# The tiles of running maxima of units 1 to 3, initialised by VectorE in place of GpSimd

## The chip, the cores and the metric

The kernel runs on one core of one Trainium2 chip. The metric is the device time in microseconds of one execution; the median of several executions is given, and one more execution is recorded by the hardware profiler. TensorE (PE in the profile) multiplies matrices, VectorE (DVE) reduces and does elementwise work, ScalarE (ACT) evaluates functions and copies, GpSimd (POOL) does elementwise work on the on-chip memory, and SyncE's queue (SP) issues the DMAs. Each engine works through its own queue in order, and engines wait for each other by semaphores.

## The reference

A transformer block with adaptive layer normalisation, in float32, for 2048 tokens of width 448, with 16 heads of 28:

```python
mod = (silu(c) @ w_mod).reshape(1, 6, 1, -1)            # sa, ca, ga, sb, cb, gb
h = layernorm(x) * (1 + ca) + sa
q, k, v = split_heads(h @ wqkv)                          # 16 heads, Dh = 28
p = softmax(q @ k^T * Dh ** -0.5)                        # per head, 2048 x 2048
x = x + ga * ((p @ v) @ wo)
h = layernorm(x) * (1 + cb) + sb
y = layernorm(h)
x = x + gb * (gelu(y @ w1 + b1) @ w2 + b2)               # 448 -> 1792 -> 448
```

## The kernel before

Every large product is made from two parts of each operand, a rounded one ("hi") and the remainder ("lo"), in three matmuls. The 16 heads are four groups `g` of four heads, and the 2048 tokens are four blocks `b` (or `qt` for queries, `cch` for keys) of 512. A **unit** is one pair (g, qt), number 4 g + qt: the attention of four heads for 512 queries.

The softmax needs the largest score of each query before the exponentials. The kernel computes these in a pass of its own: for a unit, a query row block `i`, a head `j` and a key block `cch` there is one matmul 128 x 512 (`max_mm`, line 544), and VectorE reduces its result to one column of the tile `mxp` of that unit, [128, 4, 4, 4] float32, 64 elements per partition (`max_one`, line 549). When all are there, `max_fin` reduces `mxp` over the key blocks (line 589). The tile is set to -3.0e38 when the unit's first matmul is written (lines 538 to 541); unit 0's is not.

For units 1 to 3 (`paired`) the key blocks 0 and 1 go together, in `pair_diff`: with the difference of the two key blocks (`k_diff`, tile `raw`) one matmul gives the difference of scores, ScalarE takes its positive part into a tile `slot_d`, `slot_d0h` or `slot_d0i` (line 557), a second matmul gives the scores of block 0, and one VectorE instruction adds the two and takes the maximum (line 561, in the profile a custom instruction and a read of its accumulator into `mxp`).

The **first phase**, up to about 170 us, goes over the token blocks `b` (line 894). For each, TensorE runs tasks of eleven matmuls (line 464): queries or keys of one group (`qk_task`, result `pa`), then four tasks of values (`v_task`, weights `slot_e`), then the queries and keys of group 0 of the next block. After each task comes a group of matmuls for maxima (`emit_task`, line 764), four to six of them, in five or six PSUM buffers named `ma`, `m` and `o`. In between, ScalarE copies results out (lines 500 and 526) and rounds them (503), and GpSimd subtracts for the remainder (507), which the DMA queue sends off (510). For the next block's input, GpSimd normalises transposed rows (`xn`, lines 333 and 334), ScalarE applies scale and shift (361, into a buffer `full`, of which there are three) and rounds (345), and GpSimd makes the remainder (347 and 349). These operands are `slot_b` for block 2 and `slot_c` for block 3. The second phase runs attention proper (lines 1408, 1453, 1466), the last the output projection and the MLP.

The order on every engine is the order in which the program is written, and the pools decide which buffer a tile gets.

Of the kernel before, what the change touches and what calls it, by code (L numbers as in the profile page):

```python
# [47 lines left out]
def tile_adaln_block(ctx: ExitStack, tc: tile.TileContext, x, x_t, wqkv, wo, w1, b1, w2, b2, c, w_mod, out):  # L48
    nc = tc.nc
    pe, act, dve, pool, sp = nc.tensor, nc.scalar, nc.vector, nc.gpsimd, nc.sync  # L50
# [31 lines left out]
    def sbt(tag, shape, dt=F32, bufs=1):  # L82
        return sb.tile(shape, dt, tag=tag, name=nm(tag), bufs=bufs)
# [445 lines left out]
    mxp = {}  # L529
# [4 lines left out]
    paired = ((0, 1), (0, 2), (0, 3))  # L534
    px_no = [0]

    def max_mm(g, qt, i, j, k, ps=None):
        if (g, qt) not in mxp:
            mxp[(g, qt)] = sbt("mxp", [128, 4, 4, 4], bufs=6)
            if (g, qt) != (0, 0):  # L540
                (pool if (g, qt) in paired else dve).memset(mxp[(g, qt)], -3.0e38)
        m = (ps or ps_mx)()
        js = slice(32 * j, 32 * j + DH)
        pe.matmul(m, qh_sb[(g, qt)][js, i * 128 : (i + 1) * 128], k[js, :], start=True, stop=True)  # L544
        return m

    def max_one(g, qt, cch, i, j, ps=None):
        m = max_mm(g, qt, i, j, kh_sb[(g, cch)], ps)
        dve.tensor_reduce(out=mxp[(g, qt)][:, i, j, cch : cch + 1], in_=m, op=ALU.max, axis=AX.X)  # L549
# [3 lines left out]
    def pair_diff(g, qt, i, j):  # L553
        m = max_mm(g, qt, i, j, k_diff[0])
        r = d0(1 + px_no[0] % 3)
        px_no[0] += 1
        act.activation(r, m, AF.Relu)

        def rest(ps):
            m = max_mm(g, qt, i, j, kh_sb[(g, 0)], ps)  # L560
            dve.tensor_tensor_reduce(
                out=r, in0=m, in1=r, scale=1.0, scalar=-3.0e38, op0=ALU.add, op1=ALU.max,
                accum_out=mxp[(g, qt)][:, i, j, 1:2],
            )

        return rest
# [849 lines left out]
    for u in range(NU):  # L1416
        g, qt = divmod(u, NB)
# [193 lines left out]
```

## Time and profile before

| | us |
|---|---|
| median of 3 runs | 1093.62 (1092.92 to 1094.41) |
| profiled execution | 1093.22 |
| its span, first to last instruction | 1091.4 |
| TensorE busy | 1079.4 (99%) |
| VectorE busy | 800.5 (73%) |
| ScalarE busy | 691.8 (63%) |
| GpSimd busy | 251.7 (23%) |

The page lists for each engine its busy time, then forty slices of the span in tenths (with `PEclk`, the clock granted to TensorE), then the chain that ended last: the work followed back from the last instruction, at each step to what released it. A row of the timeline gives start, duration, engine, line, operation, and the tiles as out<-in; in brackets the idle time of the engine before it and the releaser. Times in a row of a stretch are its length and each engine's busy time in it (PE, PEld, DVE, ACT, POOL), then the clock, the DMA share and GB/s.

### The profile page before, as it was taken

To read this page: it belongs to the slowest core of one execution; us is meant where nothing else is said; L and a number is where in the kernel's file an instruction comes from. 1 tells how busy PE (TensorE), PEld (TensorE's weight loads), DVE (VectorE), ACT (ScalarE), POOL (GpSimd) and SP (SyncE) were. 2 spreads that over 40 slices of the span, in tenths; PEclk is the share of its full clock that TensorE was granted. 3 is DMA by queue.
4 is the path that set the end of the run, shared out by engine and by line. 5 is a ranking of instruction groups with operands and counts; after the bars stand their busy time and mean duration, and the time that the engine had idled before them with its cause. 6 is when DMAs were issued, how large, how long until landed. Compare 5 with 4: busy or idle time off the path is not lost.

```text
span 1091.4 us, 20645 instructions
## 1 busy us (share of the span) xinstructions
PE 1079.4 (99%) x8199; PEld 657.1 (60%) x8199; DVE 800.5 (73%) x1371; ACT 691.8 (63%) x870; POOL 251.7 (23%) x231
## 2 busy tenths in 40 slices
PE   8999899999999999999999999999999999999998
PEld 6766675444444444444444444544488888888887
DVE  6978688989989898988888988585745565464322
ACT  4645658888888888888888888687943321211111
POOL 1584630011011011025231410216114032061000
PEclk9999899999999999999999999999999999999999
DMA  9454262122121311143322423111343301102000
GB/s 314 171 185 128 78 207 87 44 65 57 51 76 51 87 28 58 53 121 96 95 65 78 128 64 99 57 32 56 115 130 96 104 35 40 34 34 73 34 1 34
DMA packets 60759, 91.73 MB, mean 84 GB/s; under 512 B 14159, under 2 KB 26086, under 8 KB 60650
## 3 DMA queue, kind: packets, MB, share of 16 engines
q1 hardware_dynamic: 60178, 89.67, 26.6%
q8 instruction: 64, 1.05, 0.4%
q10 hardware_dynamic: 148, 0.46, 0.1%
q14 instruction: 33, 0.27, 0.1%
q0 software_dynamic: 336, 0.28, 0.1%
HBM read 62.54 MB, written 29.51 MB: 84 GB/s over the span
## 4 chain that ended last, share of the span: by engine, by line
PE 95%; DVE 2%; DMA 1%; ACT 1%; issue 1%; POOL 1%; SPq 0%; ACTq 0%; POOLq 0%; DVEq 0%
PE s L1453 24%; PE o L1408 23%; PE m L464 16%; PE pa L464 8%; PE m L544 7%; PE s L1545 3%; PE s L1547 3%; PE s L1546 3%; PE s L544 2%; PE ma L544 1%; DVE mxp L549 1%; PE t L1547 1%; PE t L1545 1%; PE t L1546 1%; DMA slot_c<-in_w_mod_dram 1%
## 5 line engine op out<-in xcount | busy, mean ns | idle before, releaser
L549 DVE TENSOR_REDUCE mxp<-m 128x1 f32<-128x512 f32 x583 | 376.3, 686 | 76.5 <-PE m L544 59.6
L1453 PE MATMUL s<-slot_b,slot_a 28*128 28x512 f32 (+1 forms) x3072 | 358.4, 425 | 0.1
L1453 PEld LDWEIGHTS s<-slot_b,slot_a 28*128 28x128 f32 (+1 forms) x3072 | 211.5, 183 | 175.2 <-ACT slot_c L1466 97.4
L544 PE MATMUL m<-kh,qh 28*128 28x512 f32 x607 | 221.6, 472 | 0.4 <-ACT full L840 0.3
L1466 ACT ACTIVATE slot_c<-s 128x1024 f32<-128x1024 f32 x170 | 174.8, 1028 | 52.3 <-PE s L1453 51.3
L1408 PE MATMUL o<-slot_c,v 128*32 128x512 f32 x680 | 178.9, 605 | 0.0
L1501 ACT ACTIVATE full<-m,b_col 128x512 f32<-128x512 f32 x56 | 38.6, 690 | 193.5 <-PE m L464 193.5
L757 DVE TENSOR_REDUCE mxp<-s 128x2 f32<-128x1024 f32 x107 | 131.2, 1226 | 5.7 <-PE s L544 0.8
L1408 PE MATMUL o<-slot_c1h,v 128*32 128x512 f32 x512 | 134.7, 605 | 0.0
L1408 PE MATMUL o<-slot_c0h,v 128*32 128x512 f32 x508 | 133.6, 605 | 0.0
L1466 ACT ACTIVATE slot_c1h<-s 128x1024 f32<-128x1024 f32 x128 | 130.7, 1021 | 0.0
L1466 ACT ACTIVATE slot_c0h<-s 128x1024 f32<-128x1024 f32 x127 | 130.6, 1028 | 0.0
L1466 ACT ACTIVATE slot_d<-s 128x1024 f32<-128x1024 f32 x86 | 88.4, 1028 | 27.0 <-PE s L1453 26.3
L1128 POOL TENSOR_TENSOR osb<-osb,osb 128x512 f32<-128x512 f32 x16 | 20.6, 1286 | 343.3 <-DMA osb<-drec 306.2
L544 PEld LDWEIGHTS m<-kh,qh 28*128 28x128 f32 x607 | 88.5, 182 | 15.5 <-DVE mxp L549 13.0
L1504 DVE CAST hi<-full 128x512 fp32r<-128x512 f32 x42 | 19.1, 455 | 101.7 <-ACT full L1501 101.7
L1408 PE MATMUL o<-slot_d,v 128*32 128x512 f32 x344 | 90.5, 605 | 0.4 <-ACT osb L1372 0.4
L1505 DVE TENSOR_TENSOR lo<-full,hi 128x512 fp32r<-128x512 f32 x56 | 46.2, 825 | 29.3 <-ACT hi L1504 25.3
L464 PE MATMUL m<-y,slot_a 128*128 128x512 f32 x160 | 59.7, 389 | 0.0
L721 DVE CUSTOM_DVE_ANT_0 slot_d0i<-m,slot_d0i 128x512 f32<-128x512 f32 x55 | 38.0, 692 | 16.2 <-PE m L544 12.2
L1408 PEld LDWEIGHTS o<-slot_c,v 128*32 128x32 f32 x680 | 24.5, 108 | 39.8 <-issue 37.9
L544 PE MATMUL s<-kh,qh 28*128 28x512 f32 x214 | 47.2, 436 | 0.0
(366 smaller groups left out, 1827.5 us busy)
## 6 DMA issues: line engine op xcount, KB each, us to landing
slot_b<-d SPq DMA_DIRECT2D x32, 256.0 KB
slot_a<-d SPq DMA_DIRECT2D x32, 256.0 KB
d<-lo SPq DMA_DIRECT2D x28, 256.0 KB
d<-hi SPq DMA_DIRECT2D x16, 256.0 KB
osb<-drec SPq DMA_DIRECT2D x15, 256.0 KB
out_dram<-xn SPq DMA_DIRECT2D x16, 224.0 KB
raw<-in_B_w_dram SPq DMA_DIRECT2D x14, 224.0 KB
qh<-d SPq DMA_DIRECT2D x12, 256.0 KB
```

The source lines that it names most:

```text
L464: pe.matmul(p, a, b, start=(i == 0), stop=(i == len(terms) - 1))
L544: pe.matmul(m, qh_sb[(g, qt)][js, i * 128 : (i + 1) * 128], k[js, :], start=True, stop=True)
L549: dve.tensor_reduce(out=mxp[(g, qt)][:, i, j, cch : cch + 1], in_=m, op=ALU.max, axis=AX.X)
L757: dve.tensor_reduce(out=mxp[(g, qt)][:, i, j : j + 2, cch], in_=t, op=ALU.max, axis=AX.X)
L1408: pe.matmul(o[32 * j : 32 * j + 32, :], v_sb[kt // 4][:, kt % 4, 4 * g + j, :], p[j // 2][:, j % 2, :], start=(kt == 0), stop=(kt == NKT - 1),
L1453: pe.matmul(s2[:, jj, :], ks[rows_, kp, kc], qs[rows_, qp, :], start=(term == 0), stop=(term == 2))
L1466: act.activation(pt[hf], s2, AF.Exp, scale=SCALE)
L1501: act.activation(gf, p, AF.Gelu_apprx_tanh, bias=b1_col[:, i : i + 1])
L1505: dve.tensor_tensor(out=glo, in0=gf, in1=f(ghi), op=ALU.subtract)
L1545: pe.matmul(pp, ghi[:, ts], w_hi, start=(m == 0), stop=False)
L1546: pe.matmul(pp, ghi[:, ts], w_lo, start=False, stop=False)
L1547: pe.matmul(pp, glo[:, ts], w_hi, start=False, stop=(m == NFT - 1))
```

## The change

`max_mm` sets the tile `mxp` of every unit but 0 with VectorE; before, it used GpSimd for units 1 to 3.

```diff
@@ max_mm
         if (g, qt) not in mxp:
             mxp[(g, qt)] = sbt("mxp", [128, 4, 4, 4], bufs=6)
             if (g, qt) != (0, 0):
-                (pool if (g, qt) in paired else dve).memset(mxp[(g, qt)], -3.0e38)
+                dve.memset(mxp[(g, qt)], -3.0e38)
```

Three instructions move from one queue to the other. The middle one is that of unit 2 (g = 0, qt = 2), its tile `mxp_1370`, at the last query task of block 2. On GpSimd it stands between the subtractions for two tasks:

```order
 L334 TENSOR_TENSOR xn_1090<-xn_1090,slot_v_295_1231 128x512
 L507 TENSOR_TENSOR lo_1348<-full_1347,hi_1346 128x512
-L541 MEMSET mxp_1370 128x64
 L507 TENSOR_TENSOR lo_1392<-full_1391,hi_1390 128x512
 L333 TENSOR_TENSOR xn_1130<-xn_1130,slot_v_295_1231 128x512
```

GpSimd goes from one subtraction straight to the next. On VectorE, with what each instruction waits for in brackets (`Pool`, `PE`, `Activation` and `DVE` are the semaphores of GpSimd, TensorE, ScalarE and VectorE), the place is the group of maxima in which unit 2 begins:

```order
 L561 ISA slot_d_18_101,mxp_817<-o_1343,slot_d_18_101 128x512 [waits PE_49,Activation_49]
 L561 ISA mxp_817 128x1
+L541 MEMSET mxp_1370 128x64
 L549 TENSOR_REDUCE mxp_433<-m_330_1378 128x1 [waits PE_49]
 L549 TENSOR_REDUCE mxp_433<-m_331_1381 128x1 [waits PE_49]
-L561 ISA slot_d0h_102,mxp_1370<-ma_1384,slot_d0h_102 128x512 [waits PE_49,Activation_49,Pool_49]
+L561 ISA slot_d0h_102,mxp_1370<-ma_1384,slot_d0h_102 128x512 [waits DVE_49,PE_49,Activation_49]
 L561 ISA mxp_1370 128x1
```

The memset stands at the head of the group, two reductions ahead of the first instruction that writes the tile of unit 2, and that instruction waits for VectorE's own semaphore in place of GpSimd's. The rows of TensorE, ScalarE and the DMA queue are the same in both kernels. In the two groups of maxima after this one, and at the first value task of block 2 between them, some of TensorE's waits for a PSUM buffer name another engine than before:

```order
 L544 MATMUL m_341_1421<-kh_291_1215,qh_73_341 128x512 [waits DVE_49]
-L544 MATMUL ma_1424<-kh_87_379,qh_278_1165 128x512 [waits Activation_49]
+L544 MATMUL ma_1424<-kh_87_379,qh_278_1165 128x512 [waits DVE_49]
 L544 MATMUL o_1427<-kh_87_379,qh_278_1165 128x512 [waits DVE_49]
-L464 MATMUL pa_1453<-slot_e_38_144,slot_b_228_961 128x448
+L464 MATMUL pa_1453<-slot_e_38_144,slot_b_228_961 128x448 [waits Activation_49]
```

Here the second `ma` of the group after waits for VectorE where it waited for ScalarE.

## The prediction, written before the changed kernel ran

> **What bounds the kernel now.** I read the page's busy times first, then its slices and the chain that ended last.
>
> ```profile
> span 1091.4 us, 20645 instructions
> PE 1079.4 (99%) x8199; PEld 657.1 (60%) x8199; DVE 800.5 (73%) x1371; ACT 691.8 (63%) x870; POOL 251.7 (23%) x231
> PEclk9999899999999999999999999999999999999999
> PE 95%; DVE 2%; DMA 1%; ACT 1%; issue 1%; POOL 1%; SPq 0%; ACTq 0%; POOLq 0%; DVEq 0%
> ```
>
> TensorE sets the end: it is busy 99% of the span and holds 95% of the chain. So an edit on VectorE and GpSimd counts only where TensorE waits, or runs slow, because of it. One slice of 27 us, the fifth (109 to 136 us), has a lower granted clock than its neighbours, and one of the three removed memsets lies in it. The groups of the edited line show all fifteen memsets.
>
> ```profile
> L541 DVE MEMSET mxp<- x12: 112/112/112, 43.2 to 682.2; 128x64 f32 x12
> L541 POOL MEMSET mxp<- x3: 147/147/148, 60.5 to 143.2; 128x64 f32 x3
>   DVE slot_d0h L561: 3.9, 1
> ```
>
> Twelve already run on VectorE at 0.112 us, three on GpSimd at 0.147 us, and VectorE waited 3.9 us for one of the three. The chain of waits in order of time shows what that did:
>
> ```profile
> 109.02 1.25 POOL lo L507
> 110.27 1.26 POOL xn L333
> ...
> 111.61 1.27 POOL xn L334
> 112.87 1.22 POOL lo L507
> 114.09 0.10 POOL mxp L541
> ...
> 114.22 0.04 DVE slot_d0h L561
> ...
> 114.92 0.60 DVE slot_d0i L561
> ...
> 115.58 0.79 PE o L544
> ```
>
> GpSimd is here behind with its queue: four elementwise operations of about 1.25 us stand directly ahead of a memset that itself needs no data. That memset, of the tile of unit 2, releases VectorE, and VectorE releases TensorE. The timeline of that stretch, engine by engine:
>
> ```profile
> 108.96 0.60 ACT L557 ACTIVATE slot_d0h<-ma 128x512 f32<-128x512 f32 x1 [1.16 <-PE m L544]
> 109.03 1.29 DVE L549 TENSOR_REDUCE mxp<-m 128x1 f32<-128x512 f32 x2 [0.87 <-PE m L544]
> 111.80 0.49 PE L544 MATMUL ma<-raw,qh 28*128 28x512 f32 x1
> 112.97 0.50 PE L544 MATMUL ma<-kh,qh 28*128 28x512 f32 x1 [0.67 <-ACT slot_d L557]
> 114.03 0.15 POOL L541 MEMSET mxp<- 128x64 f32 x1
> 114.22 0.69 DVE L561 CUSTOM_DVE_ANT_0 slot_d0h<-ma,slot_d0h 128x512 f32<-128x512 f32 x1 [3.90 <-POOL mxp L541]
> 115.58 0.79 PE L544 MATMUL o<-kh,qh 28*128 28x512 f32 x1 [2.11 <-DVE mxp L561]
> ```
>
> TensorE idles 0.67 + 2.11 = 2.78 us. The stall has a second part, seen in the granted clock by short windows (the last three columns are clock, DMA share and GB/s):
>
> ```profile
> 114.25:114.50 0.25, 0.00 (x0) 0.00 (x0) 0.25 (x1) 0.00 (x0) 0.25 (x1) 1.00 0.00 0
> 114.75:115.00 0.25, 0.00 (x0) 0.00 (x0) 0.25 (x3) 0.00 (x0) 0.25 (x1) 0.50 0.17 66
> 121.00:121.25 0.25, 0.25 (x4) 0.20 (x2) 0.00 (x0) 0.00 (x0) 0.25 (x1) 0.50 0.57 213
> 121.50:122.00 0.50, 0.50 (x5) 0.30 (x2) 0.40 (x1) 0.47 (x1) 0.50 (x1) 1.00 0.15 57
> ```
>
> The clock falls to 0.50 between 114.50 and 114.75, during the idle time, and is back after 121.25: some 6.7 us at half rate.
>
> **The change, part by part.** *The wait for the memset of unit 2.* I price it from the distance between the groups of matmuls for the maxima, each of which opens with one `ma<-raw`; between two groups lies one task of TensorE.
>
> ```profile
> 120.71 0.79 PE L544 MATMUL ma<-raw,qh 28*128 28x512 f32 x1
> 124.12 0.49 PE L544 MATMUL ma<-raw,qh 28*128 28x512 f32 x1
> 127.20 0.49 PE L544 MATMUL ma<-raw,qh 28*128 28x512 f32 x1
> 130.30 0.49 PE L544 MATMUL ma<-raw,qh 28*128 28x512 f32 x1
> ```
>
> Undisturbed, a value task with its maxima takes 3.08 to 3.10 us (124.12 to 127.20 to 130.30). The two from 111.80 to 124.12 are of the same kind and took 12.32 us, 6.14 more than 2 x 3.09. Of the 6.14, 2.78 are the idle time. The rest is half rate: from 115.58 to about 121.4 TensorE works 5.8 us for 2.9 us of matmuls, and some 0.4 us is left for refilling.
>
> After the change nothing of GpSimd holds the VectorE instruction that ran at 114.22. Its other two sources are the matmul `ma`, in a group opened one task earlier, and ScalarE's `slot_d0h`, done at 108.96 + 0.60 = 109.56. The new wait on VectorE's own memset is met as the memset now stands ahead of the two reductions of 109.03, where VectorE is idle 0.87 us, so its 0.112 us is hidden there (without that cover it costs 0.11). The reductions end about 110.3, the two L561 instructions about 111.6, before the 111.80 group, which then goes through without a pause. The whole 6.14 us is on the path, so the gain is 6.14 if nothing else is late.
>
> *What is late next.* GpSimd does not get earlier: its backlog only shrinks by the memset, 0.15 us at most. TensorE comes 6.14 us earlier, to the query task whose operands GpSimd still makes:
>
> ```profile
> 122.11 1.29 POOL L334 TENSOR_TENSOR xn<-xn,slot_v 128x512 f32<-128x512 f32 x1
> 124.48 1.29 POOL L347 TENSOR_TENSOR slot_c<-full,slot_c 128x512 fp32r<-128x512 f32 x1 [1.08 <-ACT slot_c L345]
> 127.61 1.28 POOL L347 TENSOR_TENSOR slot_c1h<-full,slot_c0h 128x512 fp32r<-128x512 f32 x1 [1.83 <-ACT slot_c0h L345]
> 130.74 1.29 POOL L349 TENSOR_TENSOR slot_c0h<-full,slot_c0h 64x512 fp32r<-64x512 f32 x1 [1.84 <-ACT slot_c0h L345]
> 133.15 0.62 PE L464 MATMUL pa<-slot_c0h,slot_a 128*128 128x512 f32 x2
> ```
>
> Before, GpSimd finished the normalisation of the last chunk at 123.40 and then idled ahead of each remaining step, waiting on ScalarE. Run without gaps, from 123.3, the three steps of about 1.25 us end at 127.0. TensorE's matmul on the last of them, at 133.15, moves to 133.15 - 6.14 = 127.0. They meet: a loss of 0 to 0.3 us, and I take 0.1. The gaps of 1.08, 1.83 and 1.84 us on GpSimd are thus what pays for the gain; were they not there, 4.75 us of it would be lost. ScalarE has to feed these steps:
>
> ```profile
> 124.12:127.20 3.08, 3.08 (x18) 2.28 (x17) 2.48 (x6) 2.80 (x6) 1.29 (x1) 1.00 0.00 0
> ```
>
> In an undisturbed task it is busy 2.80 of 3.08 us (the fourth column after the length), so it keeps up. It starts late, though:
>
> ```profile
> 115.97 0.82 ACT L361 ACTIVATE full<-xn,cols 128x512 f32<-128x512 f32 x1
> 117.20 0.63 ACT L345 CAST slot_c<-full 128x512 fp32r<-128x512 f32 x1
> ```
>
> The buffer `full` of this first chunk comes free only when GpSimd's operation of 112.87 ends, at 114.09. The chunk's work on ScalarE, 115.97 to 117.83, is then done at about 116.0, some 0.6 us after the point at which the next group (near 114.9) wants ScalarE. At 0.28 us of slack a task that is made up within three tasks; a group's buffers are wanted again only 3.1 us later, so the lag eats slack and not the path.
>
> *The memsets of units 1 and 3.* On VectorE they add 0.112 us each, in front of idle time:
>
> ```profile
> 65.15 0.69 DVE L549 TENSOR_REDUCE mxp<-ma 128x1 f32<-128x512 f32 x1 [1.37 <-PE m L544]
> 144.41 1.89 DVE L549 TENSOR_REDUCE mxp<-m 128x1 f32<-128x512 f32 x3 [0.32 <-PE m L544]
> ```
>
> The first run of reductions is followed by 1.37 us of idle time, and the third memset falls into the 0.32 us. Each is hidden; exposed, together, they would cost 0.22 us. What GpSimd saves there, 0.15 us each, nobody waits for: only one wait for a memset is on record. Bounds of these two: -0.3 to +0.22, taken as 0. No DMA, matmul or order on TensorE, ScalarE or the DMA queue changes, so all that follows 127 us moves forward as a block.
>
> **Sum.** -6.14 + 0.1 = -6.0 us. The profiled execution took 1093.22 us (span 1091.4), which becomes 1087.2. It lies 0.40 below the median of the three runs, 1093.62, so the predicted median is 1087.6. Runs differ by 1.5 us (1092.92 to 1094.41); 0.2%, about what a measurement of this kernel tells from no change, is 2.2 us.
>
> **A rule against the full gain.** In the rows the clock fell after 0.67 and 2.11 us of idle time, broken by one matmul. The Trainium skill, "TensorE: Matmul & The Clock Gate", section "HAM oscillation — how this bites in real kernels", has it that gaps must exceed about 3.4 us before the clock is throttled. By that rule these gaps would not be the cause, and the half rate would come regardless; the rows disagree, since the clock falls inside the gap and in no other slice, so I let the measurement decide and keep the rule's case as a rival.
>
> **The rivals.**
> - *GpSimd is the next bound.* It works without a gap from 109 us on and meets TensorE with no slack at 127.0. If its steps start 1 to 2 us later than I put them (ScalarE late with one of the three, or a buffer released late), TensorE idles that long: gain 4 to 5 us, 1088.6 to 1089.6. For it: the lack of slack. Against: the gaps of 1.83 and 1.84 us were waits for ScalarE work that TensorE's own delay had made late. Chance 0.13.
> - *The half rate stays.* Only the 2.78 us of idle time goes: 1090.8. For it: no second such drop shows cause and effect. Against: the clock fell within the gap. Chance 0.04.
> - *Another wait takes its place, or the edit doesn't take effect.* 1093.6. Against: the other sources were ready 4.6 us before, and the order has no memset left on GpSimd. Chance 0.05.
> - *Slower.* GpSimd is late for the query task at 127.0 by so much that TensorE idles as long as now (2.78 us) and its clock halves again: 2.78 + 3.36 us, all of the gain. From a delay of 2.8 us on the kernel is slower, by about the excess; a delay of 6 us would give 1096.8. That needs GpSimd's ten or so operations between 114 and 127 us to take a fifth longer each, which no row hints at. Chance 0.03.
>
> **How the numbers follow.** My forecast, the full gain, has 0.75. Faster by over 0.2% are it, the GpSimd case and the half-rate case: 0.92. Within 0.2%: 0.05. Slower: 0.03. The range goes below by the runs' spread and GpSimd's 0.15 (1086.6) and above takes in the GpSimd case with the spread (1090.0).
>
> **What would show it.** Right: VectorE's L561 no longer waits for L541; TensorE has no idle time at 112 to 116 us; the granted clock reads 1.00 through the fifth slice; groups 3.1 us apart from 111.8 on; the query task's first matmul near 124.8 in place of 130.96. Wrong: a new idle time of TensorE around 127 us with GpSimd's L349 as its releaser, or a half-rate stretch at another place.

## The result, and the profile after

| us | before | after |
|---|---|---|
| median, 6 runs each | 1093.93 (1092.92 to 1095.36) | 1087.82 (1086.50 to 1089.13) |
| profiled execution | 1093.22 | 1088.08 |
| span | 1091.4 | 1086.3 |

The ratio is 0.9944, with a 95% interval of 0.9931 to 0.9957: 6.1 us less. The page of the changed kernel, its totals and the clock by slices:

```profile
span 1086.3 us, 20646 instructions
PE 1077.9 (99%) x8199; PEld 656.5 (60%) x8199; DVE 801.0 (74%) x1374; ACT 691.2 (64%) x870; POOL 251.2 (23%) x228
PEclk9999999999999999999999999999999999999999
```

VectorE has three instructions more and GpSimd three fewer, by 0.5 us each way, and the fifth slice of the clock is a 9 like its neighbours. The edited line, and then the place of the old stall in the timeline of VectorE and TensorE:

```profile
L541 DVE MEMSET mxp<- x15: 112/112/112, 43.5 to 677.2; 128x64 f32 x15
```

```profile
108.33 0.11 DVE L541 MEMSET mxp<- 128x64 f32 x1
109.24 1.29 DVE L549 TENSOR_REDUCE mxp<-m 128x1 f32<-128x512 f32 x2 [0.80 <-PE m L544]
110.45 0.68 DVE L561 CUSTOM_DVE_ANT_0 slot_d0h<-ma,slot_d0h 128x512 f32<-128x512 f32 x1
112.01 0.49 PE L544 MATMUL ma<-raw,qh 28*128 28x512 f32 x1
115.10 0.49 PE L544 MATMUL ma<-raw,qh 28*128 28x512 f32 x1
118.20 0.49 PE L544 MATMUL ma<-raw,qh 28*128 28x512 f32 x1
121.29 0.49 PE L544 MATMUL ma<-raw,qh 28*128 28x512 f32 x1
124.40 0.49 PE L544 MATMUL ma<-raw,qh 28*128 28x512 f32 x1
127.89 0.73 PE L464 MATMUL pa<-slot_c0h,slot_a 128*128 128x512 f32 x2 [0.46 <-POOL slot_c0h L349]
128.55 0.50 PE L544 MATMUL ma<-raw,qh 28*128 28x512 f32 x1
```

The memset runs in 0.11 us where VectorE waits for TensorE anyway, and the first L561 follows the reductions at once. The groups stand 3.09 to 3.11 us apart from 112.01 to 124.40, where before the first two steps took 12.32 us. Then TensorE has the wait at GpSimd's L349.

Against the rows of before the gain can be followed group by group. Both profiles reach the group of unit 2's second step nearly together (111.80 before, 112.01 after). The one that stood at 124.12 is at 118.20, 5.92 us earlier, 6.13 counted from the group at 112. The one at 130.30 is at 124.40, 5.90 earlier. The next one stood here:

```profile
133.69 0.49 PE L544 MATMUL ma<-raw,qh 28*128 28x512 f32 x1
```

It is now at 128.55, 5.14 earlier, and 5.1 is what the span has gained. So of 6.13 us, 0.76 were given back at GpSimd's next late step, and 0.21 is the later start. The medians, 6.1 us apart, are of runs whose spread is 2.4 to 2.6 us.

### The profile page after: what moved, and what is told of

It is laid out like the page before. It is cut to its first block, busy times and chain, and to the rows that moved or that the text cites. A ratio compares the mean times of both kernels' runs of the same rounds, so it can differ in the third digit from the quotient of the medians.

```text
span 1086.3 us, 20646 instructions
## 1 busy us (share of the span) xinstructions
PE 1077.9 (99%) x8199; PEld 656.5 (60%) x8199; DVE 801.0 (74%) x1374; ACT 691.2 (64%) x870; POOL 251.2 (23%) x228
## 4 chain that ended last, share of the span: by engine, by line
PE 87%; ACT 0%; issue 0%; DVE 0%; ACTq 0%
PE s L1453 24%; PE o L1408 23%; PE m L464 17%; PE m L544 6%; PE s L1545 3%; PE s L1547 3%; PE s L1546 3%; PE pa L464 2%; PE s L544 2%; PE t L1547 1%; PE t L1545 1%; PE t L1546 1%; PE ma L544 0%; PE m L340 0%; DVE mxp L549 0%
```

## The experiments

Each kernel was timed beside the kernel before on the same chip. In three of them unit 2's memset, the engine and the place in the queue are told apart.

**Unit 2 alone on VectorE.**

```diff
-(pool if (g, qt) in paired else dve).memset(mxp[(g, qt)], -3.0e38)
+(pool if (g, qt) in ((0, 1), (0, 3)) else dve).memset(mxp[(g, qt)], -3.0e38)
```

> Only the memset of unit 2 goes to VectorE; those of units 1 and 3 stay on GpSimd. Theory A (the memset of unit 2 stood behind a backlog on GpSimd and held VectorE and TensorE): the whole gain, 6 us below the kernel before, 1087.6 to 1088.2, with no wait for L541 and the clock at 1.00 through 109 to 136 us. Rival B (GpSimd relieved of work, or VectorE's memset being the cheaper, 0.035 us each): a third of the gain or less, 1092 or more.

Measured: 1087.41 us against 1093.41, ratio 0.9945 (0.9932 to 0.9959). The whole gain. In its profile two memsets are on GpSimd as before, VectorE waits for neither, and TensorE has the same small wait for L349 (0.43 us). Rival B falls.

**Units 1 and 3 on VectorE, unit 2 on GpSimd.**

```diff
+(pool if (g, qt) == (0, 2) else dve).memset(mxp[(g, qt)], -3.0e38)
```

> Only the memsets of units 1 and 3 go to VectorE; that of unit 2 stays on GpSimd. Theory A: no change beyond 0.3 us, the wait of 3.9 us and the half-rate stretch stay. Rival B: two thirds of the gain, some 4 us.

Measured: 1093.94 against 1093.41, ratio 0.9999 (0.9990 to 1.0008). Nothing. Its profile has the stall again, and larger, from the lists of waits of VectorE and TensorE:

```profile
DVE slot_d0h L561 <- POOL mxp L541: 5.7, 1, 5.7
PE o L544 <- DVE mxp L561: 4.0, 1, 4.0
PE ma L544 <- ACT slot_d L557: 0.7, 1, 0.7
```

**All three on GpSimd, but early.** The tiles of units 1 to 3 are made and set when unit 0's is made.

```diff
+for n in [(0, 0), *paired] if (g, qt) == (0, 0) else [(g, qt)]:
+    mxp[n] = sbt("mxp", [128, 4, 4, 4], bufs=6)
+    if n != (0, 0):
+        (pool if n in paired else dve).memset(mxp[n], -3.0e38)
```

> All three memsets stay on GpSimd, but are issued when the tile of unit 0 is made, near 30 us, far ahead of the backlog. Theory A (the place in the queue matters and not the engine): the whole gain, 1087.6 to 1088.3. Rival B (the engine matters): no gain, 1093.9. Rival C (the gain comes from the waits that changed with VectorE's new instruction): no gain either.

Measured: 1088.29 against 1093.41, ratio 0.9953 (0.9939 to 0.9966). The gain is there with GpSimd doing the work (the line number is one higher in this kernel):

```profile
L542 POOL MEMSET mxp<- x3: 147/147/147, 33.2 to 33.4; 128x64 f32 x3
```

So the place in the queue made the stall, and not the engine. Rivals B and C fall.

**Where GpSimd's backlog comes from.** The kernel before, with the statistics of the last block's normalisation one task earlier; no memset is moved.

```diff
-n_stat = n - (7, 6, 99)[b]
+n_stat = n - (7, 5, 99)[b]
```

> The kernel before, memsets on GpSimd as they were, but the statistics of the last block's normalisation one task earlier, so that the rows GpSimd waits for (4.6 us of idle time until 106.4 us) are sent off before the keys of group 0 and come some 3 us earlier. Theory A (GpSimd's backlog, which starts at that wait, is what made the memset late): the memset comes near 111 us, VectorE waits under 1 us for it, no half-rate stretch, and most of the gain appears with no memset moved: 1087.2 to 1089. Rival B (the engine of the memset matters): no gain, 1093.4 or so.

Measured: 1087.27 against 1093.19, ratio 0.9938 (0.9925 to 0.9950), all of the gain. GpSimd's first normalising step, which waited until 106.36 before, and VectorE's wait for the memset:

```profile
102.72 1.30 POOL L333 TENSOR_TENSOR xn<-xn,slot_v 128x512 f32<-128x512 f32 x1 [1.41 <-DMA slot_v<-ln_dr]
110.45 0.15 POOL L541 MEMSET mxp<- 128x64 f32 x1
110.64 0.69 DVE L561 CUSTOM_DVE_ANT_0 slot_d0h<-ma,slot_d0h 128x512 f32<-128x512 f32 x1 [1.43 <-POOL mxp L541]
```

The rows and the memset come 3.6 us earlier (2.5 counted from the groups of this profile, which itself runs 1.1 us ahead there). A wait of 1.43 us in place of 3.90 leaves TensorE one listed pause of 0.20 us and the clock at full rate; the group concerned takes 1.1 us longer than undisturbed (110.68 to 114.89), and TensorE does not wait for L349 afterwards. VectorE's wait was expected under 1 us; that was a miss, and it cost the 1.1 us of this group, though the time fell within the range expected. Theory A holds: the DMA that GpSimd waited for made the backlog, and the backlog made the memset late.

**Filling TensorE's idle time.** The kernel before, with the wait kept and nine matmuls put where TensorE idled longest.

```diff
 for x, op in enumerate(ops):
+    if fill[0] and x == len(ops) - 1:       # last query task of block 2
+        held.append(ps_s())                 # the next value task's buffer
+        for _ in range(9):
+            pe.matmul(held[0], wq[0][0](0)[:, 0:128], hT[2][0](0), start=True, stop=True)
     op(...)
```

> The kernel before, with the wait kept, and nine matmuls of 0.225 us put on TensorE ahead of the last matmul of the group at 111.8 us, where it idled 2.11 us; their result is overwritten. Theory A with the half rate caused by the idle time: the clock stays at 1.00, the 2.78 us are still lost (as idle time or as filling), and the half rate's 3.36 us are gained: 1090.3 to 1090.9 against 1093.9. Rival D (the half rate comes regardless of the idle time): the clock drops all the same, and the time is 1093.9 or a little more.

Measured: 1092.01 against 1093.41, ratio 0.9991 (0.9981 to 1.0001): 1.4 us by the medians and 1.0 by the ratio, where 3.0 to 3.6 were expected, and not clear of no change. The stretch of 109 to 136 us, in the filled kernel and then in the kernel before (sixth number after the length: the clock):

```profile
109.00:136.00 27.00, 26.09 (x134) 18.09 (x134) 17.54 (x42) 17.82 (x32) 20.00 (x19) 1.00 0.23 86
```

```profile
109.00:136.00 27.00, 24.22 (x111) 17.12 (x110) 16.75 (x39) 17.35 (x32) 18.03 (x18) 0.87 0.21 79
```

Whether the half rate comes from the idle time is settled by this: VectorE still waits 4.3 us for the memset, TensorE still does no useful work meanwhile, and the clock stays at 1.00 in this stretch. Rival D falls. The amount was wrong. One reason is the size of the term (next section). Two more lie elsewhere in the execution. At the start of the kernel TensorE waits 1.64 us for a DMA, and the clock falls at 8.29 us and is back at 11.70, where the kernel before has full rate in its profile:

```profile
8.17 1.64 PE L385 MATMUL pa<-slot_c,slot_d 128*32 128x448 f32 x4 [1.64 <-DMA slot_c<-in_w_mod_dram]
8.25:8.50 0.25, 0.25 (x2) 0.06 (x3) 0.18 (x1) 0.25 (x1) 0.00 (x0) 0.57 1.10 380
11.50:11.75 0.25, 0.25 (x4) 0.00 (x1) 0.00 (x0) 0.00 (x0) 0.00 (x0) 0.60 1.08 430
```

Four of the eleven runs of the filled kernel, the profiled one among them, have a mean clock of 0.997 or 0.998 and took 1092.91 to 1094.74 us; the other seven, at 0.999 or 1.00, took 1090.82 to 1092.08. The third reason is a wait of 0.66 us which this kernel has at the first score matmul of the attention phase, and the kernel before has not. The control takes the same buffer at the same place and issues no matmul into it (`range(0)`):

> The kernel before with the buffer of the filling matmuls taken at the same place, but none of them issued: a control for the filled kernel, whose profile had a new wait of 0.66 us at the first matmul of the attention phase. If the buffers' new order makes that wait: 0.66 us above the kernel before, about 1094.0 to 1094.3, with the half-rate stretch as before. If the filling itself made it: no wait there, and the time of the kernel before. The filling's own worth is then the difference between the two, 2.2 us by the distance of the groups in the filled kernel's profile.

Measured: 1093.85 against 1093.35, ratio 1.0002 (0.9990 to 1.0013), with no wait at that matmul. So the order of the buffers alone does not make the 0.66 us. Nor does such a wait need the filling: in the profiles of unit 2 alone and of the changed kernel with earlier rows (below), the same matmul waits 0.21 and 0.15 us for the DMA `slot_b<-full`. In these three profiles that DMA was issued 1.57 to 1.75 us ahead of the last group of maxima before the matmul, in the kernel before and in the control 2.3 us. This points to the DMA, but the filled kernel's profile names ScalarE (L526), and which of the two was late there stays open. By the two ratios the filling is worth 1.2 us, in place of the 2.2 us by the groups; the intervals overlap. This control also has a half-rate stretch of another length, which is used below.

**What GpSimd still costs.** The changed kernel, with the statistics one task earlier as above:

> The changed kernel with the same edit. Theory E (GpSimd's remaining backlog is the next bound, TensorE's wait of 0.46 us for L349 at 127.9 us and the time around it): that wait goes, 0.5 to 0.8 us below the changed kernel, 1086.9 to 1087.3 where the changed kernel has 1087.6. Rival F (nothing of GpSimd is left on the path): no change against the changed kernel.

Measured: 1086.49 against 1093.19, ratio 0.9930 (0.9918 to 0.9942). GpSimd's last step for the query task now waits for ScalarE, and TensorE's matmul on it for nobody:

```profile
103.74 1.29 POOL L333 TENSOR_TENSOR xn<-xn,slot_v 128x512 f32<-128x512 f32 x1 [1.90 <-DMA slot_v<-ln_dr]
124.06 1.28 POOL L349 TENSOR_TENSOR slot_c0h<-full,slot_c0h 64x512 fp32r<-64x512 f32 x1 [0.73 <-ACT slot_c0h L345]
126.49 0.63 PE L464 MATMUL pa<-slot_c0h,slot_a 128*128 128x512 f32 x2
```

The other edit on the changed kernel takes 0.33 us off the backlog: GpSimd's two memsets of block 2's value tile are written in block 3.

```diff
 def v_init(i):
     ...
-    pool.memset(v_sb[i][:, :, :, DH : DH + 1], 1.0)
-    pool.memset(v_sb[i][:, :, :, DH + 1 : 32], 0.0)
+    if i != 2:
+        v_fill(i)                            # for block 2: at the first task of block 3
```

> The changed kernel with GpSimd's two memsets of the value tile of block 2 (0.33 us at 118.5 us) put off until block 3, behind the backlog. Theory E: L349 ends 0.33 us earlier and TensorE's wait at 127.9 us falls from 0.46 to 0.1 us: 0.3 us below the changed kernel, which the time can hardly tell but the profile can. Rival F: the wait stays.

Measured: 1087.08 against 1093.19, ratio 0.9941 (0.9927 to 0.9954). The time tells nothing, as expected; in the profile TensorE's wait for L349 is gone from the list, being too short for it. TensorE still idles 0.14 us until that result is there at 127.02, and the groups around the query task are 3.83 us apart (123.92 to 127.75), against 3.39 undisturbed (130.30 to 133.69 before). So the step costs 0.44 us in place of 0.76, the 0.3 us less that were expected.

> Both edits on the changed kernel. Theory E: as with the earlier rows alone, 1086.9 to 1087.3, since these alone remove the whole wait. If the earlier rows remove only part of it, this one is 0.3 us lower still.

Measured: 1086.96, ratio 0.9932 (0.9918 to 0.9946): as the earlier rows alone.

To see whether the earlier rows beat the changed kernel, both were run once more side by side.

> The changed kernel once more, beside the next one on the same chip: 6 us below the kernel before by every theory still standing, ratio 0.994 to 0.995.

> The changed kernel with the statistics one task earlier, once more. Theory E (TensorE's wait for L349 and the time around it were still worth 0.5 to 0.8 us): a median 0.5 to 1.0 us below that of the changed kernel beside it. Rival F: the two medians within 0.3 us.

Measured: 1087.67 for the changed kernel (ratio 0.9949, 0.9934 to 0.9964) and 1086.23 with the earlier rows (ratio 0.9937, 0.9923 to 0.9950). The intervals overlap, but the medians differ by 1.4 us, all five runs with the earlier rows (1086.03 to 1086.62) lie below five of the six beside them (1086.53 to 1089.27), and the first measurements, made in different comparisons, had ratios to the kernel before of 0.9930 and 0.9944. The version with the memsets on VectorE and the earlier rows is the fastest of those run here, by about 1 us.

## Why the prediction was right

*The cause* was as read: GpSimd's backlog, the memset of unit 2 behind it, VectorE's wait, TensorE's idle time and the halved clock. The experiments show each link: unit 2 alone gives the gain, an early place in the same queue gives it, a shorter backlog gives it, and filled idle time keeps the clock.

*The main term*, 6.14 us from the distance of the groups, came out at 6.13. Its split was mis-sized. The prediction put 2.78 us on idle time, 2.9 on half rate and the remaining 0.4 on refilling. Measured from the group to the first matmul of the value task, which takes 0.66 us undisturbed (112.01 to 112.67 after the change), the rows of before give 116.30 - 111.80 - 0.66 = 3.84 us for the wait:

```profile
116.30 0.74 PE L464 MATMUL pa<-slot_e,slot_b 128*128 128x448 f32 x1
```

From there on the half rate cost the remaining 2.30. It had also slowed the one matmul ahead: 0.72 us lie between 115.58 and 116.30, and 0.42 between the same two matmuls in the filled kernel (116.74 and 117.16). So some 2.6 us are half rate in all, and some 3.5 the wait with its restart. The restart after the idle time belongs to the wait, and the filled kernel showed it: from 112.59, its value task starts at 117.16 (wait 3.91) and from there on loses nothing. The rows for the three other kernels with the wait, each from the group of the stall to the value task and to the second group after (units 1 and 3 on VectorE, buffer taken without filling, filled):

```profile
111.57 0.49 PE L544 MATMUL ma<-raw,qh 28*128 28x512 f32 x1
117.91 3.35 PE L464 MATMUL pa<-slot_e,slot_b 128*128 128x448 f32 x8
125.41 0.49 PE L544 MATMUL ma<-raw,qh 28*128 28x512 f32 x1
110.95 0.49 PE L544 MATMUL ma<-raw,qh 28*128 28x512 f32 x1
116.13 3.24 PE L464 MATMUL pa<-slot_e,slot_b 128*128 128x448 f32 x8
122.99 0.49 PE L544 MATMUL ma<-raw,qh 28*128 28x512 f32 x1
112.59 0.49 PE L544 MATMUL ma<-raw,qh 28*128 28x512 f32 x1
117.16 1.91 PE L464 MATMUL pa<-slot_e,slot_b 128*128 128x448 f32 x8
122.72 0.49 PE L544 MATMUL ma<-raw,qh 28*128 28x512 f32 x1
```

In the table, the wait's part is the first distance less 0.66 us, the sum is the whole distance less 2 x 3.09, and the half rate's part is the difference.

| profile | VectorE waits for the memset | wait's part | half rate's part | sum |
|---|---|---|---|---|
| before | 3.9 | 3.84 | 2.30 | 6.14 |
| units 1 and 3 on VectorE | 5.7 | 5.68 | 1.98 | 7.66 |
| buffer taken, no filling | 4.7 | 4.52 | 1.34 | 5.86 |
| filled | 4.3 | 3.91 | 0.04 | 3.95 |
| after | none | 0 | 0.01 | 0.01 |

*What was late next* was named rightly, GpSimd's L349 for the query task, but at 0.1 us in place of 0.76, outside the 0 to 0.3 us that the prediction allowed for it. One of its signs of being wrong did appear: idle time of TensorE around 127 us with L349 as the releaser. GpSimd's first step of the backlog and its last, with ScalarE's two waits for it:

```profile
106.89 1.30 POOL L333 TENSOR_TENSOR xn<-xn,slot_v 128x512 f32<-128x512 f32 x1 [4.97 <-DMA slot_v<-ln_dr]
126.55 1.28 POOL L349 TENSOR_TENSOR slot_c0h<-full,slot_c0h 64x512 fp32r<-64x512 f32 x1
114.70 0.81 ACT L361 ACTIVATE full<-xn,cols 128x512 f32<-128x512 f32 x1 [0.60 <-POOL lo L507]
124.01 0.81 ACT L361 ACTIVATE full<-xn,cols 128x512 f32<-128x512 f32 x1 [0.52 <-POOL xn L334]
```

The backlog began 0.53 us later in this execution (106.89 against 106.36), since the DMA came later, and ended at 127.83 in place of 127.0. TensorE lost 0.46 us idle and 0.3 us in restarting; with the value memsets later the same 0.3 us stood beside 0.14 us of idle time. In the three other profiles with this wait (unit 2 alone, early, the changed kernel again) the idle time is 0.26 to 0.52 us and the whole step 0.55 to 0.81, so the term is that and not 0.1: with no slack at all between the two, any lateness of the start goes through to TensorE. That was the prediction's first rival at a part of its size, with GpSimd 0.53 us late in place of 1 to 2. ScalarE's waits of 0.60 and 0.52 us, the first of them predicted, cost nothing.

*The memsets of units 1 and 3* were put at 0: confirmed, with 0.9999 for the two alone. *The rivals* did not occur as priced; the new wait is an eighth of the old stall, and brought no half-rate stretch. The predicted 1087.6 us stands beside 1087.82. That the median is met to 0.2 us is luck in part: the profiled execution was forecast at 1087.2 and took 1088.08, and by the profiled executions the gain is 5.1 us, by the medians 6.11. The runs' spread does not separate these.

## What to carry to other kernels

An instruction that depends on nothing can still be the last to arrive when it stands in an in-order queue behind work that waits for a DMA. Put initialisations on the engine that uses the tile, or early in the queue; which of the two did not matter here. Price a stall of TensorE by the distance between like groups of matmuls with and without it, which takes in the idle time, the restart and the lowered clock together, and look at once at what else the same backlog feeds, since that is the next bound.

## What the hardware showed

The half-rate stretch has two lengths. By the clock in short windows before, it fell at 114.62 and rose at 121.45 (0.74 and 0.61 are the means over a quarter of a microsecond):

```profile
114.50:114.75 0.25, 0.00 (x0) 0.00 (x0) 0.25 (x1) 0.00 (x0) 0.25 (x1) 0.74 0.00 0
121.25:121.50 0.25, 0.25 (x6) 0.00 (x0) 0.00 (x0) 0.00 (x0) 0.25 (x1) 0.61 0.05 16
```

That is 6.83 us. In the kernel with the buffer taken and no filling, by windows of 1 us, it fell at 115.66 and rose at 119.08:

```profile
115.00:116.00 1.00, 0.48 (x1) 0.18 (x1) 1.00 (x4) 1.00 (x3) 1.00 (x2) 0.83 0.61 227
119.00:120.00 1.00, 1.00 (x9) 0.66 (x7) 0.00 (x0) 0.00 (x0) 1.00 (x2) 0.96 0.74 287
```

That is 3.42 us, half as long, although the wait was longer. The kernel with units 1 and 3 on VectorE has the long one again, 6.8 us, and the stretch at the start of the filled kernel is a short one (8.29 to 11.70, 3.41 us). The Trainium skill, "TensorE: Matmul & The Clock Gate", section "What's actually happening", has the clock decided in free-running windows of 3413 ns; one and two of these fit the two lengths. The same section has the clock fall after at least one idle window. If that means a window without any matmul, the rows disagree: in the 3.4 us up to the fall at 114.62 TensorE idled 0.67 us and, from the end of the matmul of 112.97, 1.15 us, with that matmul between, and at the start of the filled kernel the one wait of 1.64 us was all the idle time in the 3.4 us up to the fall. Later in the filled kernel 0.67 and 0.24 us of idle time did not lower the clock; where between 0.9 and 1.6 us in a window the limit lies was not tried. The place in a window at which a stall falls thus seems to move its cost by about 1 us (1.34 to 2.30 in the table).

This may be part of why the kernel before spread over 3.2 to 4.8 us in its 9 to 21 runs of one comparison. Over the 47 runs of the three comparisons the time does go with the mean granted clock: the median is 1092.24 us at 0.998 (12 runs), 1093.33 at 0.997 (10) and 1094.07 at 0.996 (20), and the five with a lower clock took 1094.10 to 1096.31. The changed kernel's twelve runs have 0.999 or 1.00, and still spread by 2.6 to 2.7 us. Where the half rate lies in the runs without a trace is not known.
